# Chunked gated linear attention with a StarReLU MLP behind it: x by a transposing DMA, later products, the decay's row in SBUF, earlier sums and loads

## The chip, the cores and the metric

The kernel runs on one core of a Trainium2 chip. The metric is the device time of one execution in microseconds (us). Engines are called by the names of the profile: PE (TensorE, matrix products and transposes), DVE (VectorE), ACT (ScalarE), POOL (GpSimd) and SP (SyncE, which here only issues DMAs). Each engine takes its own instructions strictly in the order in which the program wrote them; engines wait for each other through semaphores.

## The reference

What is computed, cut to what matters (B, H, S, D = 4, 8, 768, 48; the MLP has d_model = 384 and d_ff = 2048):

```python
for t in range(S):                                  # per batch and head
    state = alpha[t][:, None] * state + outer(k[t], v[t])
    y[t] = q[t] @ state
x = y.transpose(0, 2, 1, 3).reshape(B * S, H * D)   # 3072 x 384
r = maximum(x @ w_in, 0)
out = (s * r * r + b) @ w_out
```

## The kernel before

The 3072 tokens are cut into 24 blocks of 128, six to a batch. All heads of a block are worked on together, two heads to a "pair" (NP = 4). A block n passes through these steps, each a small function of the kernel; the names are used throughout.

- `load(n)`: four DMAs of 192 KB on SP (alpha, k, q, v), in runs of 192 bytes. Eight buffers of each.
- `ln(n)` (ACT), `cum(n)`: the running sum of log alpha over the block by one PE product into the bank `ct_ps`, then two ACT exponentials from it, `bi_sb` (L206) and `b_sb` (L207). "Sums" in the title means these.
- `qk(n)`: two DVE products, `kb_sb` (L223) and `qb_sb` (L224).
- `vcast(n)`: v to bf16 on POOL (L189).
- `tr(n)`: eight PE transposes of qb and kb into the same bank `ct_ps` (L229) and one DVE copy `qkT` out of it (L234).
- `amat(n)`: eight PE products into `a_ps` and two DVE multiplications by the mask, `am_a` and `am_b` (L252).
- `y(n)`: `yp` on PE (`y_ps`, and the state's part `p_ps`), the ACT copy `y_bf` (L290), then `state(n)`: one DVE addition `t1` (L333, or L331 in the first block of a batch), two POOL products `sd` (L338) and one `sc` (L342) with the decay `blast`.
- `decay(n)`, called from `cum(n)` for n of 6 and above except the last block of a batch: the last row of `b_sb` goes by DMA to a row in DRAM (L215) and, when that has landed, by two DMAs with 4-byte elements (L217) to `blast`, one number to a partition. SP waits in between.
- `xt(n)`: three PE transposes of `y_bf` (L311) into one of the two banks `h_ps`, and an ACT copy from there to `xd_sb` (L317).
- `m(n, u)`, u = 0 to 3: a unit of the first MLP product, twelve PE products into one of the two `h_ps` banks (L359), Relu on ACT (L373), the square on DVE (L380, called sq here).
- `o(n, u)`, u = 0 to 3: a unit of the second product, four PE products (L397) that add up in the single bank `o_ps`. Only after u = 3 is `o_ps` read: by an ACT copy to `keep_sb` (L406, tile `w_in_st`) for blocks below 14, by a DVE addition of the bias to `out_sb` (L410) from block 14 on, and then stored. `o(n+1, 0)` overwrites the bank and has to wait for that read.
- `add_bias(n)`: a DVE addition (L436) for the kept blocks 0 to 13, and their stores, spread over the second half.

Order is written out by hand. A list `events` holds (position, function); it is sorted by position and called, and that is the program order on every engine. A block has eight positions, y(n) stands at 8n; everything else is placed relative to it. In the steady part (n of 8 and above) that is, before the change:

```python
at(p - 14.8, cum, n); at(p - 14.6, qk, n)        # c = 14.8
at(p - 10.8, tr, n);  at(p - 7.9, amat, n)
at(p, y, n);          at(p + 1.0, xt, n)
at(p - 2.5, load, n + 4)
at(p + (2.5, 3.5, 5.5, 7.5)[u], m, n, u)
at(p + (8.5, 9.5, 12.5, 14.5)[u], o, n, u)
```

Of the kernel before, what the change touches and what calls it, by code (L numbers as in the profile page):

```python
# [8 lines left out]
FP32 = mybir.dt.float32  # L9
# [5 lines left out]
def kernel(  # L15
# [12 lines left out]
    nc = tc.nc  # L28

    B, H, S, D = q.shape  # L30
    C = 128
    NCH = S // C
    NP = H // 2
    NBLK = B * NCH
# [7 lines left out]
    UNITS = 5  # L42
    assert sum(GROUPS) == NBLK
    NLD = 8
    NFIRST = 4

    ctx.enter_context(tc.manual_schedule())
    sb = ctx.enter_context(tc.tile_pool(name="sb", bufs=1))
    ps = ctx.enter_context(tc.tile_pool(name="ps", bufs=1, space=bass.MemoryType.PSUM))
    dr = ctx.enter_context(tc.tile_pool(name="dr", bufs=1, space=bass.MemoryType.DRAM))  # L50


    ct_ps = ps.tile([128, 512], FP32, name="ct_ps")
# [9 lines left out]
    def ring(name, shape, dtype, n):  # L63
        return [sb.tile(shape, dtype, name=f"{name}{i}") for i in range(n)]
# [9 lines left out]

    q_sb = ring("q_sb", [128, H, 48], FP32, NLD)
    k_sb = ring("k_sb", [128, H, 48], FP32, NLD)
    v_sb = ring("v_sb", [128, H, 48], FP32, NLD)
    al_sb = ring("al_sb", [128, H, 48], FP32, NLD)
    la_sb = ring("la_sb", [128, H, 64], BF16, 2)
    b_sb = ring("b_sb", [128, H, 48], FP32, 3)  # L80
# [4 lines left out]
    y_bf = ring("y_bf", [128, H * 48], BF16, 2)  # L85
    qkT_sb = ring("qkT", [128, 2, NP, 128], BF16, 2)
    am_sb = [ring("am_a", [128, NP, 128], BF16, 2), ring("am_b", [128, NP, 128], BF16, 2)]
    blast = ring("blast", [128, NP, 1], FP32, 3)
    row_dr = [dr.tile([1, H * 48], FP32, name=f"row_dr{i}") for i in range(3)]
    t1_sb = sb.tile([128, NP, 96], FP32, name="t1_sb")  # L90
    sc_sb = sb.tile([128, NP, 96], FP32, name="sc_sb")
    sd_sb = ring("sd_sb", [128, NP, 96], BF16, 2)
# [4 lines left out]
    xd_sb, gt_sb, first_block = [], [], []  # L97
# [19 lines left out]
    def src(t, n):  # L117
        b, c = n // NCH, n % NCH
        return t[b, :, c * C : (c + 1) * C, :].rearrange("h s d -> s h d")

    def load_one(n, dst, t):
        nc.sync.dma_start(out=dst[n % NLD], in_=src(t, n))

# [61 lines left out]
    def ln(n):  # L185
        nc.scalar.activation(out=la_sb[n % 2][:, :, 0:48], in_=al_sb[n % NLD], func=AF.Ln)  # L186

# [3 lines left out]
    def cum(n):  # L191
        la = la_sb[n % 2]
        bank = h_ps[1] if n < NFIRST else ct_ps
        cum_ps, tot_ps = bank[:, 0:384], bank[:, 400:404]
        nc.tensor.matmul(out=cum_ps, lhsT=U_bf, rhs=la[:, :, 0:48], start=True, stop=True)  # L195
        if n < NCH - 1:
            for p in range(NP):
                nc.tensor.matmul(
                    out=tot_ps[0:112, p : p + 1],
                    lhsT=la.rearrange("a h d -> a (h d)")[:, 128 * p : 128 * p + 112],  # L200
                    rhs=ones_c,
                    start=True,
                    stop=True,
                )
        cv = cum_ps.rearrange("a (h d) -> a h d", h=H)
        nc.scalar.activation(out=bi_sb[n % 2], in_=cv, func=AF.Exp, scale=-1.0)  # L206
        nc.scalar.activation(out=b_sb[n % 3], in_=cv, func=AF.Exp)  # L207
        if n < NCH - 1:
            nc.scalar.activation(out=blast[n % 3][0:112, :, 0], in_=tot_ps[0:112], func=AF.Exp)
        elif n % NCH < NCH - 1:  # L210
            decay(n)

    def decay(n):
        row = row_dr[n % 3]
        nc.sync.dma_start(out=row, in_=b_sb[n % 3].rearrange("s h d -> s (h d)")[127:128])  # L215
        for e in range(2):
            nc.sync.dma_start(  # L217
                out=blast[n % 3][64 * e : 64 * e + 48, :, 0],
                in_=row.rearrange("o (p e d) -> e d (o p)", e=2, d=48)[e],
            )  # L220

    def qk(n):
        nc.vector.tensor_tensor(out=kb_sb[n % 3][:, :, 0:48], in0=k_sb[n % NLD], in1=bi_sb[n % 2], op=ALU.mult)  # L223
# [30 lines left out]
    group_of = []  # L254
# [38 lines left out]
    a_flat = [a.rearrange("a p t -> a (p t)") for a in a_ps]  # L293
    first_banks = {("x", i): h_ps[0] for i in range(NFIRST - 1)}
    h0, h1, a0, a1 = h_ps[0], h_ps[1], a_flat[0], a_flat[1]
# [6 lines left out]
    def bank_of(what):  # L302
        if what in first_banks:
            return first_banks[what]
        nrelu[0] += 1
        return h_ps[nrelu[0] % 2]

    def xt(n):
        hp = bank_of(("x", n)).bitcast(BF16)[:, 0 : KT * C]
        for kk in range(KT):  # L310
            nc.tensor.transpose(  # L311
                out=hp[:, kk * C : (kk + 1) * C],
                in_=y_bf[n % 2][:, 128 * kk : 128 * (kk + 1)],
                identity=ident,
            )
        g, i = group_of[n]
        nc.scalar.activation(  # L317
            out=xd_sb[g][:, :, i * C : (i + 1) * C],
            in_=hp.rearrange("a (t s) -> a t s", t=KT),
            func=AF.Copy,  # L320
        )
# [141 lines left out]
    def at(pos, fn, *args):  # L463
        events.append((pos, len(events), fn, args))
# [33 lines left out]
    for pos, what in enumerate(  # L498
        [
            (ln, 0), (vcast, 0), (cum, 0), (qk, 0), (spread,), (busy, 2), (tr, 0), (ln, 1), (busy, 1), (vcast, 1), (amat, 0), (cum, 1),  # L500
            (busy, 3), (yp, 0), (qk, 1), (st, 0), (busy, 1), (tr, 1), (ln, 2), (xt, 0), (vcast, 2), (load_w_in, 0), (load_w_in, 1), (cum, 2), (busy, 1), (amat, 1),
            (busy, 3), (yp, 1), (qk, 2), (st, 1), (busy, 1), (tr, 2), (ln, 3), (xt, 1), (vcast, 3), (load_w_in, 2), (load_w_in, 3), (cum, 3), (busy, 1), (amat, 2),
            (busy, 3), (yp, 2), (qk, 3), (st, 2), (tr, 3), (xt, 2), (mr, 0, 0), (weights_out,), (amat, 3), (mr, 0, 1), (mr, 1, 0), (sq, 0, 0),
            (yp, 3), (mr, 0, 2), (mr, 0, 3), (sq, 0, 1), (xt, 3), (sq, 1, 0), (mr, 1, 1), (sq, 0, 2), (st, 3), (sq, 0, 3), (mr, 2, 0), (mr, 2, 1), (sq, 1, 1),
            (mr, 0, 4), (sq, 2, 0), (mr, 0, 5), (sq, 2, 1), (mr, 1, 2), (sq, 0, 4), (wout, 0), (mr, 2, 2), (sq, 0, 5), (mr, 0, 6), (sq, 1, 2), (o, 0, 0), (wout, 1),
            (mr, 0, 7), (sq, 2, 2), (o, 1, 0), (sq, 0, 6), (mr, 1, 3), (ln, 4), (o, 2, 0), (sq, 0, 7), (mr, 2, 3), (cum, 4), (sq, 1, 3), (o, 0, 1),
            (sq, 2, 3), (o, 1, 1), (wout, 2), (o, 2, 1), (o, 0, 2), (o, 1, 2), (wout, 3), (qk, 4), (vcast, 4), (o, 2, 2),
            (colsum, 1), (o, 0, 3), (tr, 4), (o, 1, 3), (o, 2, 3), (colsum, 2), (o, 3, 0), (amat, 4),
        ]
    ):  # L510
        at(0.1 * pos, *what)
# [12 lines left out]
    for n in range(4, NBLK):  # L524
        p = 8 * n
        if n > 4:
            f = min((n - 5) / 3.0, 1.0)
            c, t, a = 9.0 + 5.8 * f, 5.8 + 5.0 * f, 3.4 + 4.5 * f
            at(p - c - 1.9, ln, n)
            at(p - c + 0.01, vcast, n)  # L530
            at(p - c, cum, n)
            at(p - c + 0.2, qk, n)
            at(p - t, tr, n)
            at(p - a, amat, n)

        e = 0.8 if n == NBLK - 1 else 0.0
        at(p - e, y, n)
        if n + 4 < NBLK:
            at(p - 2.5, load, n + NLD - 4)
        for u in range(4):  # L540
            at(p + (2.5, 3.5, 5.5, 7.5)[u], m, group_of[n][0], u)
            at(p + (8.5, 9.5, 12.5, 14.5)[u], o, n, u)
        at(p + 1.0 - e, xt, n)
    for _, _, fn, args in sorted(events, key=lambda e: e[:2]):
        fn(*args)

# [29 lines left out]
```

## Time and profile before

| | |
|---|---|
| time, median of 3 runs | 194.7 us (194.6 to 195.86) |
| time of the profiled execution | 194.85 us |
| its span in the profile | 193.1 us |
| granted PE clock | 1.0 throughout |
| busy: PE, DVE, ACT, POOL | 180.1, 148.8, 117.2, 64.6 us |
| DMA moved | 28.74 MB, 106627 of 113453 packets under 512 B |

The span is what the profiler sees between the first and the last instruction; the 1.75 us between it and the execution's own time lie around it. Busy time is the sum of instruction durations of an engine. PE durations overlap, since matrix products are pipelined, so the time that one PE step takes from the next is read from the distance between starts. On DVE and ACT a following instruction may also start a little before the one ahead has ended.

### The profile page before, as it was taken

What the parts mean: (1) busy time and instruction counts of PE and PEld (TensorE: products, weight loads), DVE (VectorE), ACT (ScalarE), POOL (GpSimd) and SP (SyncE); (2) the same over time, 40 slices, a digit from 0 to 9 for tenths busy, and PEclk for the clock granted to TensorE, in tenths of its full rate; (3) what the DMA queues carried; (4) which work ended last, traced back from release to release, by engine and by line L of the source; (5) the groups of instructions that cost most, each with busy time, mean ns of one, the idle gap of its engine ahead of it and who ended that gap; (6) DMA issues with size and microseconds to landing.
All of it is one profiled execution on the core that took longest, in us unless ns stands there. A gap on an engine that the chain in (4) does not pass through costs nothing.

```text
span 193.1 us, 5968 instructions
## 1 busy us (share of the span) xinstructions
PE 180.1 (93%) x2380; PEld 142.9 (74%) x2380; DVE 148.8 (77%) x288; ACT 117.2 (61%) x240; POOL 64.6 (33%) x100
## 2 busy tenths in 40 slices
PE   1898797999999999999999999999999999999993
PEld 1565686765867788887887887987877888788782
DVE  5478764587568886988977996788988999997641
ACT  3364386726767586676686676776666657654540
POOL 5147841001310533641610561551302483262000
PEclk9999999999999999999999999999999999999999
DMA  6999999999995595582969558849795956333212
GB/s 127 188 186 182 153 219 312 334 175 195 189 175 91 104 163 92 79 162 47 199 92 165 98 95 142 151 87 195 145 204 145 229 123 131 123 126 122 85 41 82
DMA packets 113453, 28.74 MB, mean 149 GB/s; under 512 B 106627, under 2 KB 113426, under 8 KB 113426
## 3 DMA queue, kind: packets, MB, share of 16 engines
q1 hardware_dynamic: 111822, 26.79, 73.2%
q0 software_dynamic: 1600, 1.57, 5.5%
q8 instruction: 18, 0.29, 0.7%
q14 instruction: 9, 0.07, 0.1%
q10 hardware_dynamic: 4, 0.00, 0.0%
HBM read 25.19 MB, written 4.74 MB: 155 GB/s over the span
## 4 chain that ended last, share of the span: by engine, by line
PE 78%; DMA 6%; DVE 3%; ACT 1%; issue 1%; DVEq 0%; ACTq 0%
PE o_ps L397 29%; PE h_ps L359 28%; DMA w_out_st<-in_moe_w_out_dram 6%; PE ct_ps L229 5%; PE a_ps L244 3%; PE a_ps L397 3%; PE h_ps L311 2%; PE y_ps L272 2%; PE ct_ps L195 2%; PE a_ps L420 1%; PE y_ps L263 1%; PE p_ps L283 1%; ACT r_sb L373 1%; DVE w_out_bf L143 1%; ACT y_bf L290 0%
## 5 line engine op out<-in xcount | busy, mean ns | idle before, releaser
L373 ACT ACTIVATE r_sb<-h_ps 128x512 bf16<-128x512 f32 x90 | 53.6, 596 | 36.6 <-PE h_ps L359 34.9
L359 PEld LDWEIGHTS <-w_in_bf 128*128 128x128 bf16 x1104 | 67.8, 98 | 8.6 <-DMA w_in_bf<-in_moe_w_in_dram 1.8
L359 PE MATMUL h_ps<-xd_all,w_in_bf 128*128 128x128 bf16 (+1 forms) x1056 | 71.5, 220 | 1.3 <-DMA w_in_bf<-in_moe_w_in_dram 1.1
L397 PE MATMUL o_ps<-w_out_bf,gt_all 128*128 128x384 bf16 x336 | 68.4, 327 | 0.6 <-DVE w_out_bf L143 0.5
L380 DVE TENSOR_TENSOR gt_all<-r_sb 128x512 bf16<-128x512 bf16 x96 | 45.4, 488 | 26.1 <-ACT r_sb L373 25.3
L338 POOL TENSOR_TENSOR sd_sb<-t_sb,blast 48x192 bf16<-48x192 f32 x40 | 20.3, 508 | 78.2 <-DVE t_sb L333 46.9
L397 PEld LDWEIGHTS <-gt_all 128*128 128x128 bf16 x368 | 32.5, 98 | 16.9 <-DVE w_out_bf L143 0.8
L189 POOL CAST v_bf<-v_sb 128x384 bf16<-128x384 f32 x24 | 18.3, 763 | 32.5 <-DMA v_sb<-in_v_dram 31.9
L342 POOL TENSOR_TENSOR sc_sb<-t_sb,blast 112x384 f32<-112x384 f32 x16 | 20.6, 1289 | 1.3
L317 ACT ACTIVATE xd_all<-h_ps 128x384 bf16<-128x384 bf16 x23 | 11.3, 490 | 14.5 <-PE h_ps L311 14.5
L234 DVE COPY qkT<-ct_ps 112x1024 bf16<-112x1024 bf16 x24 | 16.4, 684 | 3.9 <-PE ct_ps L229 3.0
L252 DVE TENSOR_TENSOR am_a<-a_ps,mask 128x512 bf16<-128x512 f32 x24 | 16.4, 683 | 3.3 <-PE a_ps L244 3.3
L224 DVE TENSOR_TENSOR qb_sb<-q_sb,b_sb 128x384 bf16<-128x384 f32 x24 | 17.0, 707 | 0.0
L223 DVE TENSOR_TENSOR kb_sb<-k_sb,bi_sb 128x384 bf16<-128x384 f32 x24 | 13.7, 570 | 3.7 <-ACT bi_sb L206 3.6
L252 DVE TENSOR_TENSOR am_b<-a_ps,mask 128x512 bf16<-128x512 f32 x24 | 16.3, 680 | 0.0
L186 ACT ACTIVATE la_sb<-al_sb 128x384 bf16<-128x384 f32 x24 | 12.4, 517 | 4.1 <-DMA al_sb<-in_alpha_dram 4.0
L290 ACT ACTIVATE y_bf<-y_ps 128x384 bf16<-128x384 f32 x24 | 11.7, 489 | 4.5 <-PE y_ps L272 4.5
L229 PEld LDWEIGHTS <-qb_sb 128*112 128x112 bf16 x96 | 8.7, 137 | 5.3 <-DVE qb_sb L224 4.0
L229 PE MATMUL ct_ps<-ident,qb_sb 128*112 128x128 bf16 x96 | 10.1, 231 | 1.1 <-DVE qb_sb L224 1.1
L206 ACT ACTIVATE bi_sb<-ct_ps 128x384 f32<-128x384 f32 x20 | 9.7, 486 | 1.0 <-PE ct_ps L195 1.0
L244 PE MATMUL a_ps<-qkT 48*128 48x128 bf16 x192 | 9.8, 222 | 0.5 <-DVE qkT L234 0.4
L207 ACT ACTIVATE b_sb<-ct_ps 128x384 f32<-128x384 f32 x20 | 9.9, 496 | 0.0
(75 smaller groups left out, 195.5 us busy)
## 6 DMA issues: line engine op xcount, KB each, us to landing
al_sb<-in_alpha_dram SPq DMA_DIRECT2D x24, 192.0 KB
k_sb<-in_k_dram SPq DMA_DIRECT2D x24, 192.0 KB
q_sb<-in_q_dram SPq DMA_DIRECT2D x24, 192.0 KB
v_sb<-in_v_dram SPq DMA_DIRECT2D x24, 192.0 KB
w_out_st<-in_moe_w_out_dram SPq DMA_DIRECT2D x4, 768.0 KB
out_dram<-w_in_st SPq DMA_DIRECT2D x14, 192.0 KB
out_dram<-out_sb SPq DMA_DIRECT2D x9, 192.0 KB
w_in_bf<-in_moe_w_in_dram POOLq DMA_DIRECT2D x4, 384.0 KB, 7.3
```

The costliest lines, as they stand in the source:

```text
L189: nc.gpsimd.tensor_copy(out=v_bf[n % 3], in_=v_sb[n % NLD])
L224: nc.vector.tensor_tensor(out=qb_sb[n % 2][:, :, 0:48], in0=q_sb[n % NLD], in1=b_sb[n % 3], op=ALU.mult)
L229: nc.tensor.transpose(out=t_ps[0:112, x, p, :], in_=t.rearrange("a h d -> a (h d)")[:, 128 * p : 128 * p + 112], identity=ident,)
L234: nc.vector.tensor_copy(out=qkT_sb[n % 2][0:112].rearrange("a x p t -> a (x p t)"), in_=t_ps[0:112].rearrange("a x p t -> a (x p t)"),)
L244: nc.tensor.matmul(out=a_ps[e][:, p, :], lhsT=qkT[r0 : r0 + 48, 1, p, :], rhs=qkT[r0 : r0 + 48, 0, p, :], start=True, stop=True,)
L252: nc.vector.tensor_tensor(out=am_sb[e][n % 2], in0=a_ps[e], in1=mask4, op=ALU.mult)
L338: nc.gpsimd.tensor_tensor(out=sd[r, :, d], in0=t1_sb[r, :, d], in1=bl[r].to_broadcast([48, NP, 48]), op=ALU.mult)
L342: nc.gpsimd.tensor_tensor(out=sc_sb[0:112], in0=t1_sb[0:112], in1=bl[0:112].to_broadcast([112, NP, 96]), op=ALU.mult)
L359: nc.tensor.matmul(out=hp[:, jj * N : (jj + 1) * N], lhsT=w_in_bf[:, kk, 128 * j : 128 * (j + 1)], rhs=xd_sb[g][:, kk, 0:N], start=(kk == ...
L373: nc.scalar.activation(out=rs, in_=h_of.pop((g, u)), func=AF.Relu)
L380: nc.vector.tensor_tensor(out=gt_sb[g][:, u * 512 : (u + 1) * 512], in0=rs, in1=rs, op=ALU.mult)
L397: nc.tensor.matmul(out=op[:, 0:d_model], lhsT=gt_sb[g][:, j * N + t * C : j * N + (t + 1) * C], rhs=w_out_bf[:, j, :], start=(j == 0), sto ...
```

## The change

Four edits. (1) For blocks 9 to 21 `xt` is no longer three PE transposes and an ACT copy, but one transposing DMA on SP from `y_bf` to `xd_sb`, at position p + 0.05. (2) From block 7 on, rising over three blocks, the units of both products come later, by 2.5 positions from block 9 to 21, 1.25 for block 22, and none for block 23. (3) The decay's row no longer goes through DRAM: POOL copies the last 32 rows of `b_sb` to `brow`, with the order of the row's elements changed, right behind the exponentials, and two DMAs two positions later take row 127 from there to `blast`. (4) From block 9 on `ln`, `vcast`, `cum` and `qk` stand two positions earlier (c = 16.8) and so do the loads (p - 4.5); `tr` and `amat` stay.

```diff
@@
+    XB, XE = 9, 21
-    row_dr = [dr.tile([1, H * 48], FP32, name=f"row_dr{i}") for i in range(3)]
+    brow = ring("brow", [128, 2, 48, NP], FP32, 2)
@@ cum(n)
         elif n % NCH < NCH - 1:
-            decay(n)
+            nc.gpsimd.tensor_copy(
+                out=brow[n % 2][96:128].rearrange("s e d p -> s p e d"),
+                in_=b_sb[n % 3][96:128].rearrange("s (p e) d -> s p e d", e=2),
+            )
 
     def decay(n):
-        row = row_dr[n % 3]
-        nc.sync.dma_start(out=row, in_=b_sb[n % 3].rearrange("s h d -> s (h d)")[127:128])
+        if n < NCH - 1 or n % NCH == NCH - 1:
+            return
         for e in range(2):
-            nc.sync.dma_start(
-                out=blast[n % 3][64 * e : 64 * e + 48, :, 0],
-                in_=row.rearrange("o (p e d) -> e d (o p)", e=2, d=48)[e],
-            )
+            nc.sync.dma_start(out=blast[n % 3][64 * e : 64 * e + 48, :, 0], in_=brow[n % 2][127:128, e])
@@ xt(n)
+        if XB <= n <= XE:
+            nc.sync.dma_start_transpose(out=xd_sb[group_of[n][0]], in_=y_bf[n % 2])
+            return
@@ the events of block n
             c, t, a = 9.0 + 5.8 * f, 5.8 + 5.0 * f, 3.4 + 4.5 * f
+            if n >= XB:
+                c = 9.0 + 7.8 * f
@@
+            at(p - c + 2.0, decay, n)
@@
+        later = 2.5 * min(max((n - XB + 3) / 3.0, 0.0), 1.0) * min(max((NBLK - 1 - n) / 2.0, 0.0), 1.0)
@@
-            at(p - 2.5, load, n + NLD - 4)
+            at(p - (4.5 if n >= XB else 2.5), load, n + NLD - 4)
         for u in range(4):
-            at(p + (2.5, 3.5, 5.5, 7.5)[u], m, group_of[n][0], u)
-            at(p + (8.5, 9.5, 12.5, 14.5)[u], o, n, u)
-        at(p + 1.0 - e, xt, n)
+            at(p + (2.5, 3.5, 5.5, 7.5)[u] + later, m, group_of[n][0], u)
+            at(p + (8.5, 9.5, 12.5, 14.5)[u] + later, o, n, u)
+        at(p + (0.05 if XB <= n <= XE else 1.0) - e, xt, n)
```

## The prediction

> **What bounds the kernel now.** I read the page's busy rows first, then the forty slices, then busy time in stretches of 7 us, then the chain that ended last, then the timeline of two blocks. The first three say that PE is the bound from about 55 us to the end.
>
> ```profile
> PE 180.1 (93%) x2380; PEld 142.9 (74%) x2380; DVE 148.8 (77%) x288; ACT 117.2 (61%) x240; POOL 64.6 (33%) x100
> ...
> PE   1898797999999999999999999999999999999993
> ```
>
> ```profile
> 76.00:83.00 7.00, 7.00 (x106) 5.75 (x102) 6.23 (x11) 4.77 (x12) 3.22 (x4) 1.00 0.60 96
> ...
> 153.00:160.00 7.00, 7.00 (x103) 5.75 (x101) 6.51 (x14) 4.50 (x10) 4.03 (x4) 1.00 0.70 163
> ```
>
> A block takes some 7.04 us (y(20) starts at 153.34, y(21) at 160.38), all of it PE work; the list of waits of PE between 62 and 175 us is empty. Taking work off PE pays only if no wait enters in its place. What PE waits for when it does wait is shown once by the chain:
>
> ```profile
> 139.90 0.48 DVE out_sb L410
> 140.42 0.81 PE o_ps L397 x4
> ```
>
> A unit o(n+1,0) may not start before DVE has read o(n,3) out of the one bank. Now the order on DVE around the start of y(20):
>
> ```profile
> 153.32 0.54 DVE L410 TENSOR_TENSOR out_sb<-o_ps,bias_w 128x384 f32<-128x384 f32 x1
> 154.23 0.42 DVE L380 TENSOR_TENSOR gt_all<-r_sb 128x512 bf16<-128x512 bf16 x1 [0.37 <-ACT r_sb L373]
> 154.57 0.55 DVE L333 TENSOR_TENSOR t_sb<-p_ps,sc_sb 112x384 f32<-112x384 f32 x1
> 155.04 0.68 DVE L252 TENSOR_TENSOR am_a<-a_ps,mask 128x512 bf16<-128x512 f32 x1
> 155.64 0.68 DVE L252 TENSOR_TENSOR am_b<-a_ps,mask 128x512 bf16<-128x512 f32 x1
> ```
>
> The addition is ahead of t1 and the two masks. Each start is about 0.08 us before the end ahead (155.04 + 0.68 against 155.64), which I use below.
>
> **PE transposes removed.** The price is the distance of starts on PE, not the 0.33 us of the row:
>
> ```profile
> 126.77 0.33 PE L311 MATMUL h_ps<-ident,y_bf 128*128 128x128 bf16 x3
> ...
> 126.94 0.33 PE L195 MATMUL ct_ps<-la_sb,U_bf 128*128 128x384 bf16 x1
> ```
>
> 0.17 us, for 13 blocks: **-2.2 us**, the whole gain there is. The ACT copy (0.49 us) goes too, but ACT is busy 4.3 to 5.0 of 7 us and bounds nothing.
>
> **The new order.** Call Y the start of y(b), at position 8b. From the positions, PE in the middle blocks runs: m(b-1,2), y(b), amat(b+1), o(b-2,3), m(b-1,3), o(b-1,0), o(b-1,1), m(b,0), tr(b+2), m(b,1), o(b-1,2), cum(b+3), m(b,2). DVE runs: kb and qb of b+2, sq(b-1,2), t1(b), am_a, am_b, the addition of o(b-2,3), sq(b-1,3), sq(b,0), copy qkT(b+2), sq(b,1). PE prices by distances of starts: m 0.67, o 0.65, y with the state's part 0.64 and amat 0.33 (125.14 to 125.78 to 126.11), tr 0.45, cum 0.16. Three neighbours are new.
>
> **New wait 1: cum behind the copy of tr.** Both use `ct_ps`. Before, tr came 4 positions after cum and cum 4 after tr; now cum follows tr by 2, with only m and o between. The way from an m unit through ACT to sq:
>
> ```profile
> 144.49 0.83 PE L359 MATMUL h_ps<-xd_all,w_in_bf 128*128 128x128 bf16 x12
> ...
> 145.42 0.60 ACT L373 ACTIVATE r_sb<-h_ps 128x512 bf16<-128x512 f32 x1 [1.17 <-PE h_ps L359]
> ```
>
> So Relu starts 0.93 us after its m, and sq (146.04) ends at 1.97. In the new order the copy qkT is behind sq(b,0): it starts at 1.89, ends at 2.57, and PE goes on 0.05 later, at 2.62. PE itself is there after m, tr, m, o = 2.44. Wait 0.18 us, in some 13 blocks: **+2.4**. What is late next is bi, b, kb and qb of that block, which stand first in the chain of wait 3. Bounds: 0 if the copy passes through a free slot earlier, 0.6 where an add_bias (0.47) falls between.
>
> **New wait 2: o_ps behind the ACT copy, blocks below 14.** Between o(b-2,3) and o(b-1,0) PE had m, y and amat (1.64 us); now m alone (0.67). The copy starts 0.20 after the o unit (123.82 + 0.65 to 124.67), takes 0.49, and 0.05 pass until PE: 0.74. Wait 0.07 to 0.12, six times: **+0.6**.
>
> **New wait 3: o_ps behind the DVE addition, from block 14 on.** Here the addition is no longer ahead of the masks but behind them. Chain from cum, 0.83 before Y (cum 0.16, m 0.67): bi is written at Y + 0.07 (0.16 + 0.26 to reach ACT + 0.48). kb starts at Y + 0.11, qb 0.58 (0.55 alone, mean 0.71), sq 1.20, t1 1.55, am_a 2.02, am_b 2.62, the addition 3.22, its end 3.77, PE 3.81. PE is at o(b-1,0) already at Y + 0.64 + 0.33 + 0.65 + 0.67 = 2.29: wait 1.5 us. o(15,0) to o(22,0), eight times: **+12.0** (0.47 less where a batch ends and t1 is missing, 0.47 more where an add_bias falls into the chain). A floor comes from the masks alone: amat ends on PE at Y + 0.97, DVE can start 0.26 later, two masks and the addition need 0.60 + 0.60 + 0.55, PE resumes at 3.03: 0.74 each, 5.9 in all, however idle DVE is. The upper end: qb as slow as its slowest beside POOL (0.5 more) and add_bias in each chain (0.47): 2.5 each, 20. The middle is taken, because each of its rows is a typical one.
>
> On qb beside POOL, the row:
>
> ```profile
> 128.56 1.18 DVE L224 TENSOR_TENSOR qb_sb<-q_sb,b_sb 128x384 bf16<-128x384 f32 x1
> ```
>
> The Trainium skill (SBUF — State Buffer, on the shared port pair) says that a DVE instruction with two SBUF inputs and a GpSimd instruction that reads SBUF exclude each other for a whole instruction. The trace agrees in places (1.18 beside 0.55 here), and the mean of 0.71 says not everywhere. It speaks against the change: the new POOL copy falls beside kb and qb. By it, the same 0.63 in each of eight chains would make the sum 5 us longer.
>
> **The transposing DMA.** The trace has none. Needed: y_bf is written at Y + 1.30 (125.14 to 126.44), SP sees it 0.1 later, and PE reaches m(b,0) at Y + 2.36 + 0.65 + 0.65 = 3.66. So 2.2 us are hidden in blocks 9 to 14; in later ones wait 3 hides 1.5 more. Lower end, the quickest issue to landing in the trace, 1.5 KB:
>
> ```profile
> 165.69 0.27 SPq L215 DMA_DIRECT2D row_dr<-b_sb  x1
> 167.29 0.81 SPq L217 DMA_DIRECT2D blast<-row_dr  x2
> ```
>
> 1.6 us. Upper end, a whole load set, 5.1 (issue at 120.77, DMA share falls at 125.9), if the transpose lands only after one. The tile is 96 KB; four 192 KB loads flow in some 4 us, so half of one costs 0.5. 1.6 + 0.5 = 2.1, and a little for a longer issue: I take 2.4. Wait 0.2 in six blocks and more in block 9, whose units come up as the delay still rises: **+1.5**.
>
> **The rest.** The two-DMA decay: SP's waits for the row (32.9 us over 15) go, but nobody waits on `blast`; POOL's list names `t_sb` (46.9) and no decay. POOL's copy: nearest row vcast 0.76 (bounds 0.51 and 1.29 of sd and sc), 15 times, in the 3.7 us and more that POOL idles before each sd; if that cover were gone, sd would still have 3 us until the next y. SP now takes loads, transpose, a store and two decay issues in a block, about 3 us of issue plus the wait for y_bf; the loads start some 3.5 us before Y and flow until about Y + 1.6, the transpose's issue is at Y + 1.4, so its bytes come behind them with next to no queueing. Deferring products is neutral on a full PE: blocks 7 to 9 get shorter, the end gets the units back; there xt(23) finds less cover, **+0.7**.
>
> **Sum.** -2.2 + 2.4 + 0.6 + 12.0 + 1.5 + 0.7 = +15.0. On the profiled execution's 194.85 us (span 193.1 and 1.75 around it; the median of the runs, 194.7, is 0.15 lower): **209.9 us**.
>
> **Rivals.**
> - *Only PE's work counts* (the other side). Mechanism: the addition reaches DVE in time and the transpose is hidden, so -2.2 alone decides: 192.6. It holds if the addition ends before Y + 2.24. For it: PE's list of waits is empty now, DVE idles up to 1.7 of 7 us. Against: the floor of 3.03 above. Chance 0.05.
> - *The floor*. DVE works ahead and only the masks hold the addition: 5.9 in place of 12.0, 203.8. For: DVE's idle time; against: kb and qb can't start before cum. Chance 0.12.
> - *The shared resource of DVE and POOL* lengthens each chain by 0.63: 5 more, 214.9. For: the 1.18; against: the mean. Chance 0.10.
> - *The transpose is the bound.* At 4 us from issue to landing, blocks 9 to 15 take 1.4 + 4 + 3.4 (m(b,0) to the next y) = 8.8 in place of 7.1: seven times 1.7, less the 1.5 counted, and 0.3 in six later blocks: 222.1. For: two-byte elements, and DMA shares of 0.6 to 1.1 in the stretches of 7 us; against: the rings are drained by then. Chance 0.16.
> - *It isn't a fast transpose at all* but 49152 elements in packets of their own. The decay's 384 four-byte packets cost a share of 0.2 over 1 us on 16 engines, 8 ns each: 25 us a block, above 450 us. Against: one instruction is written for it. Chance 0.02.
>
> By the Trainium skill (Advanced Engine Details and Errata, X-Bar Transpose (TRN2)) such transposes are as fast as regular DMAs, 350 to 400 GB/s. An estimate from it is 0.28 us for 96 KB, 1.9 with the 1.6, so no wait for the DMA and 208.4; no run here shows one yet.
>
> **How the numbers follow.** The forecast has 0.55. Range 202 to 225: it takes in the floor, the longer chains and the DMA up to about 4.3 us; outside are the other side, the last rival and the far ends. A measurement of this kernel tells about 1% (2 us) from no change. The 0.05 of the first rival lies on that limit, so faster 0.03 and within 1% 0.03; slower 0.94.
>
> **What would show it.** Right: PE's waits name DVE `out_sb` at L410 before `o_ps`, some 1.5 us from about 125 us on; small ones before L195 on the copy L234; blocks of 7.1 us before y(15) and 8.5 after. Wrong: a late addition ahead of the masks, no wait at `o_ps`, blocks under 7 us; or waits of PE for `xd_all` on a DMA, which would put the loss into blocks 9 to 14.

## The result and the profile after

The changed kernel takes 219.99 us (median of four, 218.55 to 221.66) beside 195.13 us of the kernel before on the same chip: a ratio of 1.1309, 95% interval 1.1254 to 1.1365. It is slower, as forecast, and 10 us slower than the forecast of 209.9. The profiled execution took 220.64 us with a span of 218.6 us, 25.5 more than the 193.1 before. Some executions of three kernels below (two of four with the sums at their old place, two of twelve with the row alone, two of six with the second order) were in a slower state; ratios are of the others, and so are the times given with them. Line numbers have moved by three behind L311: m is L362, o L400, the bias addition L413, add_bias L439, t1 L336 (L334 where a batch begins).

The page's busy rows and slices:

```profile
PE 186.8 (85%) x2339; PEld 143.6 (66%) x2341; DVE 147.7 (68%) x288; ACT 112.0 (51%) x227; POOL 74.9 (34%) x115
...
PE   1987899999999999898799989967959696898793
...
PEclk9999699999999999999699999999997999999999
```

PE has some 40 instructions fewer and 6.7 us more of busy time: its products ran longer in places. The third row has three slices in which the granted clock, the share of full speed that PE is allowed, is well below full (0.6, 0.6, 0.7). POOL's share is up by a point, the others are down; PE now waits. From the list of PE's waits from 60 to 205 us, which was all but empty before (columns: sum in us, how many, longest; PEld rows are weight loads, which partly lie under a running product; the largest row left out, `PEld L400 <- issue` with 13.0 us, is the weight loads of o held up together with their products):

```profile
PE o_ps L400 <- DVE out_sb L413: 11.3, 7, 2.6
...
PEld L195 <- DVE qkT L234: 6.3, 13, 0.9
...
PE h_ps L362 <- DMA xd_all<-y_bf: 4.1, 4, 2.1
...
PE ct_ps L195 <- DVE qkT L234: 1.2, 3, 0.5
```

Three of the prediction's four waits are there by name: o behind the late addition, cum behind the copy of tr, m behind the transposing DMA. Wait 2, o behind the ACT copy, is too short for the list; it shows in the starts below. The chain that ended last (start, duration, what), at the place that was shown of before, now with the masks ahead of the addition:

```profile
182.02 0.60 DVE am_b L252
182.62 0.47 DVE out_sb L413
183.13 0.97 PE o_ps L400 x5
```

The timeline of one block, where y starts at 157.91; these are the rows from cum to the o unit that waits longest:

```profile
157.07 0.34 PE L195 MATMUL ct_ps<-la_sb,U_bf 128*128 128x384 bf16 x1
...
157.97 0.56 DVE L223 TENSOR_TENSOR kb_sb<-k_sb,bi_sb 128x384 bf16<-128x384 f32 x1 [0.44 <-ACT bi_sb L206]
...
158.44 1.31 POOL L211 COPY brow<-b_sb 32x384 f32<-32x384 f32 x1 [7.03 <-ACT b_sb L207]
158.44 0.55 DVE L224 TENSOR_TENSOR qb_sb<-q_sb,b_sb 128x384 bf16<-128x384 f32 x1
...
158.91 1.06 DVE L439 TENSOR_TENSOR w_in_st<-w_in_st,bias_w 128x384 f32<-128x384 f32 x1
159.22 2.04 SPq L310 DMA_TRANSPOSE xd_all<-y_bf  x1
159.37 0.83 PE L362 MATMUL h_ps<-xd_all,w_in_bf 128*128 128x128 bf16 x12
...
159.90 0.72 DVE L383 TENSOR_TENSOR gt_all<-r_sb 128x512 bf16<-128x512 bf16 x1
...
160.54 0.55 DVE L334 COPY t_sb<-p_ps 112x384 f32<-112x384 f32 x1
161.00 0.68 DVE L252 TENSOR_TENSOR am_a<-a_ps,mask 128x512 bf16<-128x512 f32 x1
...
161.60 0.68 DVE L252 TENSOR_TENSOR am_b<-a_ps,mask 128x512 bf16<-128x512 f32 x1
162.20 0.54 DVE L413 TENSOR_TENSOR out_sb<-o_ps,bias_w 128x384 f32<-128x384 f32 x1
```

DVE works through this without a hole from 157.97 to 162.74, and PE goes on at 162.79. It is the chain of the prediction's wait 3, row by row, with one add_bias in it that took 1.06 us beside POOL's copy, where it takes 0.54 alone.

For the transposing DMA, the view of its line gives the time from issue to landing, when its last bytes have arrived:

```profile
DMA to landing us min/median/max: 2.3/2.6/4.4
```

**Where the 25 us went.** I took every start of a product on PE from 60 us to the end and subtracted the usual distance of that kind in the kernel before (0.056 us in m, 0.163 in o and so on); what is left is summed by the kind of unit that came late, less the same sum for the kernel before. The wait before the o unit at 162.79, for instance, is 162.79 - 159.37 - 0.67 = 2.75.

| term | predicted | measured |
|---|---|---|
| three PE transposes a block removed | -2.2 | not separable, -2.2 kept |
| cum behind the copy of tr | +2.4 | +3.7 |
| o behind the keep copy, blocks below 14 | +0.6 | +1.1 |
| o behind the late addition, eight times | +12.0 | +13.6 (1.80, 1.50, 2.75, 2.27, 1.80, 1.29, 1.02, 1.13) |
| m behind the transposing DMA | +1.5 | +5.9 (block 9: 1.14, 11: 2.23, 14: 0.94, 17: 0.49, rest small) |
| xt(23) at the end | +0.7 | +0.7 |
| tr behind a late qb | 0 | +0.3 |
| products longer inside their units | 0 | +1.8 |
| ahead of 60 us | 0 | +0.5 |
| sum | +15.0 | +25.4 (span: +25.5) |

The -2.2 in the right column is taken over from the prediction, so that the sum closes is no test of it.

### The profile page after: what moved, and what is told of

Its sections match the earlier page's. It is cut to its first block, busy times and chain, and to the rows that moved or that the text cites. A ratio compares the mean times of both kernels' runs of the same rounds, so it can differ in the third digit from the quotient of the medians.

```text
span 218.6 us, 5875 instructions
## 1 busy us (share of the span) xinstructions
PE 186.8 (85%) x2339; PEld 143.6 (66%) x2341; DVE 147.7 (68%) x288; ACT 112.0 (51%) x227; POOL 74.9 (34%) x115
## 4 chain that ended last, share of the span: by engine, by line
PE 56%; DVE 14%; DMA 12%; ACT 6%; SPq 4%; issue 4%; POOL 2%; ACTq 0%; DVEq 0%; POOLq 0%
PE h_ps L362 22%; PE o_ps L400 16%; DMA xd_all<-y_bf 7%; SPq L122 4%; ACT r_sb L376 4%; PE ct_ps L229 4%; DMA w_in_bf<-in_moe_w_in_dram 3%; DVE am_b L252 3%; PE a_ps L400 2%; DVE gt_all L383 2%; PE ct_ps L195 2%; DMA v_sb<-in_v_dram 2%; PE a_ps L244 2%; DVE am_a L252 2%; DVE qb_sb L224 2%
## 5 line engine op out<-in xcount | busy, mean ns | idle before, releaser
L383 DVE TENSOR_TENSOR gt_all<-r_sb 128x512 bf16<-128x512 bf16 x96 | 47.9, 504 | 49.3 <-ACT r_sb L376 48.4
L362 PE MATMUL h_ps<-xd_all,w_in_bf 128*128 128x128 bf16 (+1 forms) x1056 | 76.1, 224 | 5.3 <-DMA xd_all<-y_bf 4.1
L362 PEld LDWEIGHTS <-w_in_bf 128*128 128x128 bf16 x1104 | 71.1, 100 | 14.3 <-issue 5.9
L400 PE MATMUL o_ps<-w_out_bf,gt_all 128*128 128x384 bf16 x336 | 67.3, 330 | 12.3 <-DVE out_sb L413 12.3
L400 PEld LDWEIGHTS <-gt_all 128*128 128x128 bf16 x368 | 33.5, 99 | 30.8 <-issue 14.2
L211 POOL COPY brow<-b_sb 32x384 f32<-32x384 f32 x15 | 20.4, 1360 | 62.2 <-ACT b_sb L207 62.1
L189 POOL CAST v_bf<-v_sb 128x384 bf16<-128x384 f32 x24 | 14.2, 590 | 23.9 <-DMA v_sb<-in_v_dram 22.5
L345 POOL TENSOR_TENSOR sc_sb<-t_sb,blast 112x384 f32<-112x384 f32 x16 | 14.0, 876 | 1.3
L224 DVE TENSOR_TENSOR qb_sb<-q_sb,b_sb 128x384 bf16<-128x384 f32 x24 | 14.1, 588 | 0.0
L229 PE MATMUL ct_ps<-ident,qb_sb 128*112 128x128 bf16 x96 | 10.3, 234 | 1.7 <-DVE qb_sb L224 1.7
L229 PE MATMUL ct_ps<-ident,kb_sb 128*112 128x128 bf16 x96 | 9.9, 229 | 0.0
```

The source lines that it names most:

```text
L189: nc.gpsimd.tensor_copy(out=v_bf[n % 3], in_=v_sb[n % NLD])
L211: nc.gpsimd.tensor_copy(out=brow[n % 2][96:128].rearrange("s e d p -> s p e d"), in_=b_sb[n % 3][96:128].rearrange("s (p e) d -> s p e d", ...
L224: nc.vector.tensor_tensor(out=qb_sb[n % 2][:, :, 0:48], in0=q_sb[n % NLD], in1=b_sb[n % 3], op=ALU.mult)
L229: nc.tensor.transpose(out=t_ps[0:112, x, p, :], in_=t.rearrange("a h d -> a (h d)")[:, 128 * p : 128 * p + 112], identity=ident,)
L362: nc.tensor.matmul(out=hp[:, jj * N : (jj + 1) * N], lhsT=w_in_bf[:, kk, 128 * j : 128 * (j + 1)], rhs=xd_sb[g][:, kk, 0:N], start=(kk == ...
L383: nc.vector.tensor_tensor(out=gt_sb[g][:, u * 512 : (u + 1) * 512], in0=rs, in1=rs, op=ALU.mult)
```

## The experiments

My theory after this: the late addition is the largest part, as forecast; the transposing DMA costs about four times what was counted, because it lands behind loads; and the clock, which the prediction left out, falls behind long waits. Rivals: the DMA is innocent and only shifts the waits; POOL's copy slows DVE; or the clock falls for a reason of its own.

**x back on PE.** All else as in the changed kernel.

```diff
-        if XB <= n <= XE:
-            nc.sync.dma_start_transpose(out=xd_sb[group_of[n][0]], in_=y_bf[n % 2])
-            return
...
-        at(p + (0.05 if XB <= n <= XE else 1.0) - e, xt, n)
+        at(p + 1.0 - e, xt, n)
```

> The change with x of blocks 9 to 21 back on PE (at p + 1.0), all else as changed. Theory A (the new order: o_ps waits behind the masks and the late addition, ct_ps behind the copy of tr): the waits at o_ps and before L195 stay, the landing waits go, 2.2 us of PE work come back: 211 to 214 us, blocks of 7.0 to 7.4 us up to y(15) and 8 to 9.5 us behind it. Theory B (the transposing DMA's landing is most of the loss): 200 us or less. Theory C (the POOL copy of the row slows DVE): about as slow as the change, 216 to 220 us.

Measured: 214.42 us, ratio 1.1039 (1.0978 to 1.1100), 0.4 us above the expected range. The waits of PE (L397 and L410 are here what L400 and L413 are in the changed kernel):

```profile
PE o_ps L397 <- DVE out_sb L410: 11.5, 8, 2.4
PEld L195 <- DVE qkT L234: 6.6, 15, 0.9
```

Both waits that come from the order stay at their size with no transposing DMA in the kernel. The DMA accounts for 5.6 us of the changed kernel (219.99 - 214.42), where the prediction had it as a small gain (-2.2 + 1.5). That is its cost beside the other waits, which hide a part of it.

**o at its old place.** The later m stays.

```diff
-            at(p + (8.5, 9.5, 12.5, 14.5)[u] + later, o, n, u)
+            at(p + (8.5, 9.5, 12.5, 14.5)[u], o, n, u)
```

> The change with the units o back at 8.5, 9.5, 12.5, 14.5 while the units m stay 2.5 positions later, so that the addition of o(n,3) is ahead of the masks again. Theory A: PE's waits for DVE out_sb at o_ps vanish (11.3 us and the half clock behind them), the DMA's landing is no longer hidden from block 16 on: 200 to 207 us. Theory B: what is hidden by the wait at o_ps now shows as wait for the DMA, 213 us or more. Theory C: about 216.

Measured: 209.71 us, ratio 1.0766 (1.0701 to 1.0831). That is 10.3 us less than the changed kernel, and above the expected 200 to 207. The wait at `o_ps` is gone from the list; in its place stands the DMA:

```profile
PEld L362 <- DMA xd_all<-y_bf: 10.5, 11, 2.5
PE h_ps L362 <- DMA xd_all<-y_bf: 7.4, 6, 2.2
```

By the same sum over starts, m is late by 4.1 us more here than in the changed kernel, and o by some 14 us less. So the late o costs some 14 us by itself, and 4 of them had been hiding the DMA, which is what the prediction said of it ("wait 3 hides 1.5 more").

**Sums at their old place, alone and with o early.**

```diff
-            if n >= XB:
-                c = 9.0 + 7.8 * f
```

> The change with ln, vcast, cum and qk back at c = 14.8, all else as changed. Theory A: the wait of cum for the copy of tr (7.5 us in the change's list for PE and its loads) goes, kb and qb leave the chain ahead of the late addition, whose wait shrinks to about 0.9 us a block: 204 to 209 us. Theory B: no gain, 218 or more. Theory C: the POOL copy falls elsewhere on DVE, 214 to 220.

> Both of these: o early and sums back; what is left of the change is the transposing DMA with m 2.5 positions later, the row in SBUF and the earlier loads. Theory A: only the landing beyond 2.2 us is left, less 2.2 us of PE work: 195 us at a landing of 2.3 us, 198 at 2.6, 203 at 3.0. Theory B: 208 or more. Theory C: 205 or more, with DVE instructions longer than before.

Measured: 225.80 us, ratio 1.1603 (1.1548 to 1.1657), and with o early 222.46, ratio 1.1434 (1.1391 to 1.1477). The times missed, and on the wrong side: undoing part of the change made it slower. The wait of cum for the copy of tr did go, as expected: neither list of PE's waits has it. What stands there is the DMA; from the kernel with o early, the row and the timeline of block 9:

```profile
PE h_ps L362 <- DMA xd_all<-y_bf: 20.1, 9, 4.2
```

```profile
82.61 0.52 SPq L122 DMA_DIRECT2D al_sb<-in_alpha_dram  x1
...
83.53 0.48 ACT L290 ACTIVATE y_bf<-y_ps 128x384 bf16<-128x384 f32 x1
...
84.52 0.83 SPq L122 DMA_DIRECT2D v_sb<-in_v_dram  x1
...
85.45 1.52 SPq L310 DMA_TRANSPOSE xd_all<-y_bf  x1
...
89.14 0.83 PE L362 MATMUL h_ps<-xd_all,w_in_bf 128*128 128x128 bf16 x12 [2.86 <-DMA xd_all<-y_bf]
```

Two things are late here. `y_bf` is written at 84.01, but SP is still issuing the set of loads, and the transpose goes out only at 85.45. And it lands 3.7 us after that in place of 2.3, 0.5 us behind the last of that set, whose first DMA had been issued 2.8 us ahead of it. Over the thirteen blocks the issue comes 0.4 to 3.9 us behind `y_bf` in seven, 13 us in all (in the two longest cases stores stand ahead of it as well); in the changed kernel it is 1.3 us in one block and 0.03 in the others, and the set is issued 4.5 us ahead or more. What moved the loads is the decay: its two DMAs stand two positions behind cum, so with c = 14.8 they come 3.2 positions after a y instead of 1.2. On SP they wait there for POOL's copy, and the loads, at 3.5 positions after that y, are queued behind them. One edit (the row in SBUF) and another (the earlier sums) are tied to each other on SP: what one costs depends on the other.

**Loads earlier still**, once with o early and the sums at their old place, once with o early alone.

```diff
-            at(p - (4.5 if n >= XB else 2.5), load, n + NLD - 4)
+            at(p - (6.5 if n >= XB else 2.5), load, n + NLD - 4)
```

> As the kernel with o early and sums back (222.5 us), and the loads at p - 6.5 instead of p - 4.5, so that SP issues them ahead of the decay's two DMAs and they have left the DMA rings when the transpose is issued. Theory A, mended (a transpose issued behind loads lands only after them; in empty rings it lands 2.3 us after its issue): the long landings go, PE's waits for xd_all fall to some 0.3 us a block, the blocks of 10 to 12 us between blocks of 7 vanish: 197 to 201 us. Theory B, in the form that is left (a transpose beside the kernel's work is slow whatever is in front of it): no change, 219 to 223 us.

> The changed kernel with o back at p + 8.5 to 14.5 and the loads two positions earlier still (p - 6.5), the sums left at p - 16.8. Theory A (with the o wait gone, the rest is the transpose that lands late behind a load set on the DMA rings): moving the loads away from the transpose brings the median landing to 2.3 us, PE's waits for xd_all below 5 us, and the time from 209.7 to 200 to 205. Theory B (the landing is late for another reason): 208 to 211, waits as in the kernel with o early alone.

Measured: the first 206.81 us, ratio 1.0648 (1.0593 to 1.0703); the second 209.72, ratio 1.0784 (1.0743 to 1.0826). The first is 6 us above the expected range, though the same four DMAs two positions earlier take 15.6 us off the 222.46: the issues are late by 6 us in all in place of 13, and the median landing goes from 3.0 to 2.4. So the loads just ahead of the transpose, in SP's list and on the rings (the DMA engines' own lists), made up most of what undoing the sums had cost. They are not the whole: PE still waits 9.6 us for the DMA in its list, and four of the nine recorded landings take 3.0 to 4.4 us although their set had landed by 0.9 us after the issue (each has one of the packets beside it that are named further down). The first kernel, with the sums at their old place, is 2.9 us faster than the second, and `L195`, 6.4 us in the second, is gone from its list. That is near the 3.7 us of wait 1, but the order on SP differs as well. In the second the expectation missed: nothing moved against 209.71, the landings got later (median 2.9, before 2.6), and the waits stayed:

```profile
PEld L362 <- DMA xd_all<-y_bf: 11.2, 11, 2.8
PE h_ps L362 <- DMA xd_all<-y_bf: 8.5, 8, 2.4
```

Here the loads still went out 4.5 to 7.2 us ahead of the transpose, as with o early alone (4.6 to 7.0). SP takes its list in order and knows nothing of positions. With c = 16.8 the list of a block is transpose, decay, loads; moved from 3.5 to 1.5 positions after y the loads are still behind the decay at 1.2, so hardly anything on SP changed places. With c = 14.8 the same move takes them past the decay at 3.2. A position counts only where it passes another instruction of the same queue.

**The row in SBUF alone**, in the kernel before.

```diff
@@ cum(n)
-            decay(n)
+            nc.gpsimd.tensor_copy(
+                out=brow[n % 2][96:128].rearrange("s e d p -> s p e d"),
+                in_=b_sb[n % 3][96:128].rearrange("s (p e) d -> s p e d", e=2),
+            )
@@ decay(n)
...
+            nc.sync.dma_start(out=blast[n % 3][64 * e : 64 * e + 48, :, 0], in_=brow[n % 2][127:128, e])
...
@@ the events of block n
+            at(p - c + 2.0, decay, n)
```

> The kernel before with the third edit alone: POOL's copy of the decay's rows to SBUF and two DMAs from there in place of the way through DRAM. Theory A (as predicted, nobody on the path waits for it): 194 to 196, within 1% of the kernel before. Theory B (POOL's copy, measured 1.36 us in place of the 0.76 estimated, lies beside kb and qb on DVE and lengthens them by some 0.6 us in up to 15 blocks, and PE waits for qb): 198 to 204.

Measured: 195.10 us, ratio 1.0034 (1.0009 to 1.0059). This is the first theory: 0.7 us, though not nothing. POOL's copy took 1.05 us here (1.36 in the changed kernel, 0.76 estimated), and qb did not grow:

```profile
L210 POOL COPY brow<-b_sb 32x384 f32<-32x384 f32 x15 | 15.8, 1054 | 18.7 <-ACT b_sb L206 18.1
L223 DVE TENSOR_TENSOR qb_sb<-q_sb,b_sb 128x384 bf16<-128x384 f32 x24 | 15.7, 655 | 0.0
```

**The change without its three costly places**: x on PE, o and sums as before; kept are the later m, the row and the earlier loads.

> What is left of the change without its three costly places: x of all blocks on PE again, the sums at p - 14.8 and o at p + 8.5 to 14.5 as before; kept are the later m (p + 5 to p + 10), the row in SBUF and the loads two positions earlier. Theory A (the whole loss sits in the transposing DMA, the late o and the early sums): 194 to 197. Theory B (later m or earlier loads cost by themselves, as the 1 us lost between y(5) and y(8), ahead of the first transposing DMA, may hint): 198 to 204.

Measured: 196.72 us, ratio 1.0122 (1.0076 to 1.0167), inside the first theory. Of the 2.4 us left, the starts on PE show 0.85 before xt(23), 0.77 and 0.51 before two tr that waited for qb, and 0.86 at two o units. So some 23 of the 25 us are in the transposing DMA, the late o and the early sums. The kernel of 206.81 us above is this one with the DMA in it (and the loads two positions earlier): 10 us more. The DMA costs more where no other wait hides it than the 5.6 us that it adds to the changed kernel.

**Products in the gaps.** To see what the clock costs, the changed kernel got products on PE that nobody reads, at places where it waits.

```diff
+    def fill(k):
+        for _ in range(k):
+            nc.tensor.matmul(out=p_ps[:, 384:512], lhsT=U_bf, rhs=mask4[:, 0], start=True, stop=True)
...
+        if n == 11:
+            at(p + 2.5 + later - 0.01, fill, 24)
+        if 14 <= n <= 22:
+            at(p + 8.5 + later - 0.01, fill, 16)
```

> The changed kernel with extra products on PE that nobody reads: 24 of 128x128 (about 1.3 us) ahead of m(11,0), and 16 (about 0.9 us) ahead of o(n,0) for n = 14 to 22, all at places where PE waited 1.5 to 2.6 us anyway. Theory A (the long waits of PE make the granted clock fall to half behind them, and that is part of what the prediction left out): the stretches of half clock at 105 and 163 us vanish, the waits named before o_ps shrink by some 0.9 us each, and the time falls by 1.7 us for each stretch, to 216 to 218. Theory B (the clock falls for another reason): the stretches stay and the time stays at 219 to 222, or grows by the extra products.

Measured: 218.0 us, ratio 1.1218 (1.1163 to 1.1273). First the changed kernel, in stretches of 1 us behind its waits of 2.07 us (PE back at 104.91) and 2.59 us (162.79); the last three figures of a row are granted clock, DMA share and GB/s:

```profile
105.00:106.00 1.00, 1.00 (x12) 1.00 (x12) 0.00 (x0) 0.00 (x0) 0.00 (x0) 0.53 0.96 188
106.00:107.00 1.00, 1.00 (x12) 1.00 (x10) 0.03 (x1) 0.66 (x2) 0.00 (x0) 0.50 1.16 224
...
163.00:164.00 1.00, 1.00 (x5) 0.49 (x4) 0.90 (x2) 0.00 (x0) 0.15 (x1) 0.54 0.41 151
164.00:165.00 1.00, 1.00 (x4) 0.44 (x3) 0.00 (x0) 0.00 (x0) 0.00 (x0) 0.50 0.19 56
```

Then the kernel with the extra products at the same places:

```profile
106.00:107.00 1.00, 0.85 (x16) 0.85 (x16) 0.00 (x0) 0.00 (x0) 0.00 (x0) 1.00 0.14 22
107.00:108.00 1.00, 1.00 (x21) 1.00 (x20) 0.29 (x1) 0.92 (x2) 0.00 (x0) 1.00 1.09 212
...
163.00:164.00 1.00, 0.39 (x4) 0.24 (x3) 1.00 (x3) 0.00 (x0) 0.90 (x2) 1.00 0.00 0
164.00:165.00 1.00, 1.00 (x9) 0.61 (x8) 0.73 (x2) 0.00 (x0) 0.00 (x0) 1.00 0.52 192
```

Filling the gap keeps the clock: the first theory holds for the stretches. In time it is 2.0 us, at the upper edge of what was expected, and the intervals of the two ratios overlap a little. A gap that got no products, 1.99 us at block 9, was followed by a new stretch at half clock (3.4 us from 88.4), and the landings came later (median 3.2), so part of the gain went back.

**How long a gap.** The kernel before with six deliberate waits of PE: a product, then 2, 5, 8, 11, 14 or 17 ACT copies each reading the one ahead, then a product that reads the last. The extra products and copies go to tiles that nobody reads.

> The kernel before, with six waits of PE put in on purpose at positions 66, 82, 98, 114, 130 and 146: a small product, 2, 5, 8, 11, 14 and 17 dependent ACT copies, and a product that needs the last one. It measures how long a PE wait has to be for the granted clock to fall to 0.5 behind it. From the changed kernel (waits of 2.07 and 2.59 us were followed by about 3.3 us at half clock, one of 2.1 was not, those under 1.7 never): no fall after the waits below 2 us, a fall after those above 3 us. If the fall has another cause than the wait: none after any of them, or after the short ones too.

Measured (one execution, 224.14 us): the waits were 0.99, 2.01, 3.04, 4.06, 5.08 and 6.10 us.

```profile
113.36 0.23 PE L176 MATMUL p_ps<-mask,gap_sb 128*128 128x128 bf16 x1 [3.04 <-ACT gap_sb L175]
...
132.00 0.24 PE L176 MATMUL p_ps<-mask,gap_sb 128*128 128x128 bf16 x1 [4.06 <-ACT gap_sb L175]
```

```profile
115.02:118.43 3.41, 3.41 (x56) 2.97 (x54) 3.12 (x6) 2.19 (x5) 0.00 (x0) 1.00 0.30 47
...
132.08:135.50 3.42, 3.42 (x28) 2.96 (x29) 0.46 (x2) 1.20 (x2) 0.00 (x0) 0.50 1.23 209
```

After the first three the clock stayed full, after the last three it was 0.50 for 3.4, 6.8 and 6.8 us. By itself this would put the limit between 3 and 4 us; the changed kernel fell after 2.07 and 2.59 and not after 2.11. Over all kernels of this study from 30 us on, none of nine waits of 1.41 to 1.97 us was followed by a fall, 15 of 23 waits of 1.99 to 3.99 us were, by 1.6 us after PE went on, and all five from 4.06 us on. Length alone doesn't decide between 2 and 4 us.

The place of the wait does. In each of the ten executions with several changes of the granted clock from 20 us on, all changes lie on one grid of 3.413 us, whatever the waits do (in the changed kernel 105.05, 108.47, 163.08, 166.49 and 217.69 us, for instance). Four stretches of that grid in the changed kernel; behind the length of a stretch stands PE's busy time:

```profile
101.64:105.05 3.41, 1.34 (x11) 0.72 (x10) 0.74 (x2) 0.53 (x1) 0.44 (x1) 1.00 0.23 38
...
159.67:163.08 3.41, 0.82 (x12) 0.61 (x10) 3.41 (x7) 0.60 (x1) 2.36 (x5) 1.00 0.65 167
...
169.91:173.32 3.41, 1.76 (x25) 1.28 (x25) 3.41 (x7) 1.17 (x3) 3.14 (x5) 1.00 0.27 67
173.32:176.73 3.41, 2.95 (x38) 2.43 (x38) 1.00 (x3) 0.72 (x2) 0.62 (x1) 1.00 0.20 65
```

In the first two PE is idle for 2.07 and 2.59 us, and the stretch behind each is at 0.50. The last two share the wait of 2.11 us, 1.65 and 0.46, and the clock stays. The deliberate wait of 3.04 us was cut in the same way, 1.28 and 1.75. Over all fourteen kernels (where there is but one change, the grid is laid through it), from 30 us on, each of the 20 stretches at full clock with 1.99 us or more of idle PE was followed by half clock, and none of the 627 with 1.90 or less. This is read from the traces; no run moved a wait along the grid.

**Two orders that should keep what is good.** Both keep the transposing DMA and the row; sums, tr and amat are moved so that the copy of tr is not ahead of cum, o comes before the masks, and m and the loads leave the transpose more time.

```
            first                        second
sums        p - 17.3                     p - 16.8
decay       p - 14.8                     p - 14.3
tr, amat    p - 13.8, p - 8.4            p - 12.3, p - 6.4
loads       p - 7.0                      p - 6.5
m           p + 7.0, 8.0, 8.5, 9.0       p + 6.5, 8.5, 9.5, 11.5
o           p + 9.0, 10.5, 12.5, 13.0    p + 9.5, 12.0, 14.0, 15.0
```

> A new order that keeps the transposing DMA and takes away each of the waits found: in blocks 9 and on the sums at p - 17.3 and tr at p - 13.8 (cum 4.5 positions behind the tr before it), amat at p - 8.4, m at p + 7, 8, 8.5, 9, o at p + 9, 10.5, 12.5, 13 (the addition of o(n,3) is ahead of the masks, m(n,0) 7 positions after y), loads at p - 7. Theory A: PE waits for nothing, 2.2 us of PE work are gone and blocks take 6.9 us: 192 to 194 us (0.98 to 0.995 of before); where a code-loading packet of 16 KB holds up a landing, up to 1 us more. Theory B: 205 or more. Theory C (the POOL copy slows DVE in any place): 198 or more.

> The same aim with another order: sums at p - 16.8, tr at p - 12.3, amat at p - 6.4, m at p + 6.5, 8.5, 9.5, 11.5, o at p + 9.5, 12, 14, 15, loads at p - 6.5. Theory A: 192 to 194 us. Theory B: 205 or more. Theory C: 198 or more.

Measured: 200.56 and 200.28 us, ratios 1.0327 (1.0279 to 1.0375) and 1.0285 (1.0227 to 1.0343). Both missed the expected 192 to 194, and no version here beats the kernel before. The times lie in the third theory's range, that POOL's copy slows DVE in any place, but alone that copy costs 0.7 us; what it costs in these two orders was not tried. Against the changed kernel they win back 19 of 25 us by order alone. What is left in the first:

```profile
...
PEld L195 <- DVE qkT L234: 2.2, 4, 0.9
PE h_ps L362 <- DMA xd_all<-y_bf: 2.0, 3, 1.3
PEld L400 <- DVE gt_all L383: 2.0, 5, 0.7
```

These are three small waits in place of two large ones. By the sum over starts m comes 4.1 us later than in the kernel before and cum 2.5: more than the 2.2 us that the transposes on PE cost.

## Why the prediction was right, and where it was short

**What bounds the kernel, the direction, the place.** Right: PE's list of waits was empty, so the 2.2 us were all there was to win, and each wait that entered was named ahead. The rival on the other side fell with the addition behind the masks, and the floor with it: the shortest of the eight waits at o, 1.02 us, is above its 0.74. That the time fell into the range owes more to the range than to the sum, which had 15.0 of the 25.4 us.

**Wait 3.** Right in mechanism and nearly in size: 13.6 us for 12.0. The chain of rows (kb, qb, sq, t1, two masks, addition) is the one in the timeline. What lengthened it were add_bias in it and squares of 0.72 to 0.93 us where 0.42 was taken; part of that is POOL's copy (below), which the sum had left out, so the size came out close partly by luck. That o early wins only 10.3 us is no contradiction: the DMA's waits grow by 4.

**Wait 1.** Right in kind; 3.7 us for 2.4. In a quiet block cum starts 0.85 behind the o unit ahead (156.22 to 157.07) where 0.65 is usual, so 0.20 for the predicted 0.18; the rest are three places of 0.39 to 0.67. Its consequence was seen too: one late cum makes kb, qb and with them the addition of that block later.

**The transposing DMA.** This is the step that failed most: 5.9 us for 1.5. The duration was close, 2.3 us at its quickest for the estimate of 2.4. The sentence that failed is that its bytes come behind the loads "with next to no queueing", though the same sentence has the loads flow until Y + 1.6 and the issue at Y + 1.4. The prediction had named waits of PE for `xd_all` as a sign of being wrong, and they are in the list. Of thirteen landings five of the ten that carry a record were 2.8 us or later. In blocks 9, 14, 17 and 18 the set of loads was issued 4.5 to 5.1 us ahead and landed 1.9 to 3.0 us after the transpose's issue, and the transpose came 0.4 to 0.9 us behind it. That loads ahead of it make it late was shown by moving them (15.6 us). The largest, 4.4 us at block 11, had something else beside it; the DMA part of the page for 100 to 105 us:

```profile
q1 hardware_dynamic: 1739, 0.32, 43.4%
q8 instruction: 1, 0.02, 1.8%
q14 instruction: 1, 0.01, 0.6%
...
xd_all<-y_bf SPq DMA_TRANSPOSE x1, 4.4
```

Two packets of the instruction queues, of 16 and 8 KB, took 1.8% of 16 engines for 5 us (1.45 us) and 0.6% (0.5 us), each on one ring. The nine kernels with the transpose have 84 landings on record. All 13 of 4.1 us or more have such a packet of 16 KB that starts 0.8 to 2.3 us behind their issue; of those without one between the issue and 2.3 us behind it, none took more than 3.7. All 27 with one that starts 0.1 to 2.1 us behind took 3.0 or more. So next to the loads ahead of it these packets are the likely second cause; that is read from the traces, no run moved a packet. The Trainium skill (DMA: Bandwidth & Descriptors, Queues, rings and completion order) says that each DMA engine takes the descriptors of a ring in ring order. The landings 0.4 to 0.9 us behind the loads agree with it.

The rate of 350 to 400 GB/s that the prediction drew from the Trainium skill (Advanced Engine Details and Errata, X-Bar Transpose (TRN2)) led, with the 1.6 us of its rows, to an estimate of 1.9 us; the quickest landing here was 2.3 us, and the measurement decides.

The rival in which the transpose is the bound came nearer in time (222.1 us) than the forecast, but only in part in kind: blocks 9 to 15 took 8.1 us and not its 8.8, and the waits at o stayed the largest.

**Half clock.** The sum had no such term. It is some 2 us: 1.8 in the starts, 2.0 with the gaps filled. The prediction had priced each wait by its length, and 3.4 us at half clock behind it may cost 1.7 us more. The Trainium skill (TensorE: Matmul & The Clock Gate, What's actually happening) names a free-running window of about 3.4 us, and half clock after an idle one. The grid of 3.413 us agrees with the first. The second differs: here 1.99 us of idle PE in one stretch of it was enough, and the measurement decides.

**POOL's copy.** The duration was missed (1.36 us, above the upper bound of 1.29); alone, in the kernel before, the copy costs 0.7 us. The shared resource did not lengthen qb, whose mean fell from 0.71 to 0.59 us: in the timeline copy and qb start together, qb takes its 0.55, and the copy takes 1.31 where the first of the copies, beside a mask, took 0.88. What grows is the DVE instruction behind qb, a square to 0.93 (0.42 alone) or an add_bias to 1.06 (0.54 alone), and each ends 0.1 to 0.2 us behind the copy. All five chains of wait 3 that have a copy beside them show this, with waits of 1.50 to 2.75 us; the three without have 1.02 to 1.29. So the rival's mechanism did come about, in another instruction than qb and in five chains of eight: some 2.5 us of the 13.6, an estimate from five times 0.5, as no run has the changed kernel without the copy.

**The rest.** The tail is 0.7 as worked out. Blocks were forecast at 7.1 us before y(15) and 8.5 after. By the ends of `y_bf` they took 8.1 from block 9 to 15 (85.64 to 134.01 us) and 9.0 from 16 to 23 (141.39 to 204.48): the first is the DMA with its half clock, the second wait 3 with the same two. (The block that the prediction calls y(20) is y(19): L331, which begins a batch, stands one block ahead of it. No price hangs on that.) The time lies in the upper half of the range, where the DMA's upper end had been counted in.

## What to carry to other kernels

Before moving a step off a full engine, list who will be in front of each of its successors on every other queue: here 2.2 us were saved on PE, and what decided was that an addition slid behind two masks on DVE. A DMA put on the path has to be priced with what is on its rings at that moment, and its issue with what SP waits for ahead of it; moving a load by two positions was worth 15.6 us in one order and nothing in another. Some 2 us of idle PE within one stretch of 3.4 us may cost up to 1.7 us more at half clock, so several short waits apart are cheaper than one long one. And before a copy is put on POOL, look at which DVE instructions will lie beside it.

## What the runs showed of the hardware

- The transposing DMA from SBUF to SBUF, 128x384 in bf16 (96 KB): 1.2 us on SP's queue, 2.3 us from issue to landing at its quickest, up to 3.7 behind a set of loads, and up to 5.4 where a 16 KB packet of an instruction queue started 0.8 to 2.3 us behind the issue.
- The granted clock of PE changes on a grid of 3.413 us. It went to 0.50 after each of 20 stretches of the grid with 1.99 us or more of idle PE, after none of 627 with 1.90 or less, and stayed there for 3.4 or 6.8 us; products in the gap keep it at 1.00.
- Where POOL's copy lay beside qb, either the copy took longer (1.3 to 2.3 us; 0.88 beside a mask) or the square or add_bias behind qb did as well (0.93 for 0.42, 1.06 for 0.54), ending 0.1 to 0.2 us behind the copy. Masks and t1 kept their 0.68 and 0.55.
- POOL's copy of 32x384 f32 with the elements reordered: 1.05 to 1.36 us on average, up to 2.27 for one.
